# Outer term loop in split products, and separate issue of an expert's two weight transfers

## The chip, the cores and the metric

The kernel runs on one core of a Trainium2 chip. The metric is the device time of one execution in microseconds (us), the median of several executions. A core has five engines that run their own instruction streams in order and wait for each other by semaphores: TensorE (PE: matmuls, with PEld for its weight loads), VectorE (DVE), ScalarE (ACT), GpSimd (POOL) and SyncE (SP), which here issues nearly all DMA transfers.

## What is computed

Three layers follow one another: attention in which only scores close to the row's maximum count, a mixture of eight experts of which each token uses one, and a dense layer that all tokens pass.

```python
def _moe_ref(x, modality_id, w_gate, modality_bias, w1, w2):
    logits = x @ w_gate + modality_bias[modality_id]
    e_idx = np.argmax(logits, axis=1)
    ...
    for e in range(E):
        mask = e_idx == e
        h = np.maximum(x[mask] @ w1[e], 0.0)
        out[mask] = gate_w[mask, None] * (h @ w2[e])

def _moe2_ref(x, w_in, w_out):
    h = x @ w_in
    g = h * (1.0 / (1.0 + np.exp(-1.702 * h)))
    return g @ w_out
```

There are 2304 tokens of width 512. Each of the eight experts has w1 of 512 x 1024 and w2 of 1024 x 512; the dense layer has w_in of 512 x 2048 and w_out of 2048 x 512. All is fp32.

## The kernel before

**Split products.** Each fp32 operand of a product is split in two parts: a high part, rounded to the type that TensorE multiplies in one pass (float32r), and a low part, the rest. A product is then three terms: high weights with high data, high weights with low data, low weights with high data. ScalarE makes the high part (a copy that rounds), VectorE the low part (a subtraction that needs the high part).

**Expert blocks.** Tokens are sorted by expert into blocks of up to 512 rows, each of one expert. Five blocks stand in the program: four of 512 tokens and one of 264 (`SLOT_ROWS`, blocks 0 to 4 here; the code calls them slots). A block has eight steps, f = 0 to 7 (main loop, lines 1370 to 1416). Step f calls `ffn.step` (line 1025):

- `s1` (line 967), the first product: four pieces of 128 input channels (kd) times three terms, 12 matmuls of 128x128 weights with 512 columns of data (264 in the last block) into one accumulator, `tr`. Weights are ah (high) and al (low), data xh and xl.
- relu and its split, on ScalarE (hh) and VectorE (hl).
- `s2` or, in an expert block, `s2_cols` (line 1008), the second product, of the step two before (`LAG`): four groups of 128 output channels (d), each with an accumulator of its own, times three terms. Weights are bh and bl, data hh and hl.

The second product of a block's last step falls into step 1 of the next block. Behind it four evictions bring the accumulators to tiles y, and SyncE writes these to DRAM (lines 1273 and 1281).

**Weights.** They come in four pieces, g = 0 to 3, each for two steps. A piece has two transfers of 512 KB: ra (of w1, line 1227) and rb (of w2, line 1230), with two buffers each. `split(g, 0)` turns ra into ah and al (lines 1237 and 1238), `split(g, 1)` turns rb into bh and bl. At even f the loop splits the next piece's ra, `split(g + 1, 0)`, which step f + 2 uses; at odd f it splits rb of the current piece, which the second product uses in the next step. `load(g)` issues both transfers together, at odd f, two pieces ahead:

```python
            else:
                if f > 1 or not HO:
                    blk["split"](g, 1)
                if g + 2 < 4:
                    blk["load"](g + 2)
                elif nxt:
                    nxt["load"](g - 2)
```

At f = 1 `split(0, 1)` is called from inside the step (`mid`), between the first product and relu. A transfer into a buffer waits on SyncE until the split of the piece that held it is over; what stands behind it in SyncE's queue waits too.

**Other work in the same stretch.** `gather_slot` fetches the next block's rows (GpSimd), `scale` multiplies them by the gate's weight (ScalarE), `xprep` transposes and splits them, one of four pieces at a time, at the steps that `XP` gives; in blocks 0 and 1 the fourth piece comes at the very end of step 7. From block 1 on, `conv` prepares the dense layer's weights: a load of 512 KB into one of two buffers cv_raw (line 1138) in the steps that `CV` lists, ScalarE's and VectorE's bit operations one step later (from line 1144 on), and the split another step later.

**Dense layer.** Five blocks of tokens (four of 512 and one of 256) take 16 steps each, with `s1` as above on weights wi_h, wi_l and, in `s2`, h as weights and wo_h, wo_l as data (line 1000).

Of the kernel before, what the change touches and what calls it, by code (L numbers as in the profile page):

```python
# [33 lines left out]
CO = (0, 3)  # L34
CA = (0, 1, 2, 2, 2, 2, 2, 2, 2, 2, 2, 2, 2, 2, 2, 2)
CB = (0, 0, 0, 1, 0, 1, 0, 1, 0, 1, 0, 1, 0, 0, 0, 0)
HO = True
XP = ((0, 0, 0, 0, 1, 1, 1, 9), (0, 0, 0, 0, 1, 1, 1, 9), (0, 0, 0, 1, 1, 1, 9, 0))
SC = ((0, 0, 2, 2), (0, 0, 0, 4), (0, 0, 4, 0))
CV = ((), (3, 5, 7), (0, 1, 3, 4, 5, 7), (0, 1, 3, 4, 5, 7), ())  # L40
# [882 lines left out]
class Ffn:  # L923
# [43 lines left out]
    def s1(self, blk, f, mid):  # L967
        nc = self.nc
        T = blk["T"]
        wh, wl = blk["wa"](f)  # L970
        hps = self.ps_tr.tile([128, 512], F32, name="tr")
        i = 0
        for kd in range(4):
            for w, x in ((wh, "xh"), (wh, "xl"), (wl, "xh")):
                nc.tensor.matmul(hps[:, 0:T], w[:, kd, :], blk[x][:, kd, 0:T], start=(i == 0), stop=(i == 11))  # L975
                i += 1
        hh = self.hp.tile([128, 512], F32R, name="hh")
        hl = self.hp.tile([128, 512], F32R, name="hl")
        if mid:
            mid()  # L980
        self.pend.append((blk, f, hh, hl))
        return blk["act"](hps[:, 0:T], hh[:, 0:T], hl[:, 0:T])
# [25 lines left out]
    def s2_cols(self, blk, f, hh, hl):  # L1008

        nc = self.nc  # L1010
        T, last = blk["T"], blk["nf"] - 1
        if f == 0:
            sc = [self.ps_sc.tile([128, 2, 512], F32, name="sc") for _ in range(2)]
            blk["y"] = [sc[d // 2][:, d % 2, 0:T] for d in range(4)]
        wh, wl = blk["wb"](f)
        for d in range(4):
            ds = slice(d * 128, (d + 1) * 128)
            for i, (w, h) in enumerate(((wh, hh), (wl, hh), (wh, hl))):
                nc.tensor.matmul(  # L1019
                    blk["y"][d], w[:, ds], h[:, 0:T], start=(f == 0 and i == 0), stop=(f == last and i == 2))  # L1020
        if f == last:
            for d in range(4):
                blk["cols"](d, blk["y"][d])
# [16 lines left out]
def moe_kernel(ctx, tc, kq, v, tau, mid, w_gate, mod_bias, w1, w2, w_in, w_out, out):  # L1040
# [89 lines left out]
    ffn = Ffn(tc, ident, ps)  # L1130
# [81 lines left out]
    def slot(e_idx, g_rows, raw_tile, w_tile, put):  # L1212

        ev = nc.sync.value_load(e_idx, min_val=0, max_val=NE - 1)
        W = {}

        def scale(t, fast=False):

            g = g_rows[t]
            if fast:  # L1220
                nc.vector.tensor_scalar_mul(g[:, 0:DM], g[:, 0:DM], g[:, DM:DM + 1])
            else:
                nc.scalar.activation(g[:, 0:DM], g[:, 0:DM], ACTF.Copy, scale=g[:, DM:DM + 1])

        def load(g):
            ra = raw_tile("ra", "p (k f) -> p k f", dict(k=4))
            nc.sync.dma_start(
                ra, w1[bass.ds(ev, 1), :, g * 256:(g + 1) * 256].rearrange("a (kd p) f -> p (a kd) f", p=128))
            rb = raw_tile("rb", "p (g d) -> p g d", dict(g=2))
            nc.sync.dma_start(  # L1230
                rb, w2[bass.ds(ev, 1), g * 256:(g + 1) * 256, :].rearrange("a (g p) d -> p (a g) d", p=128))
            W[g] = [ra, rb]

        def split(g, i):
            raw = W[g][i]
            hi, lo = (w_tile("ab"[i] + x, ("p (k f) -> p k f", "p (g d) -> p g d")[i], (dict(k=4), dict(g=2))[i]) for x in "hl")
            nc.scalar.copy(hi, raw)  # L1237
            nc.vector.tensor_sub(lo, raw, hi.bitcast(F32))  # L1238
            W["ab"[i], g] = [hi, lo]

        def cols(d, yps):
            y, write = put(d, yps.shape[1])
            if d % 2:
                nc.vector.tensor_copy(y, yps)
            else:
                nc.scalar.copy(y, yps)
            if write:
                write(y)

        return dict(  # L1250
            nf=8, act=relu, cols=cols, scale=scale, load=load, split=split,
            wa=lambda f: [w[:, :, (f % 2) * 128:(f % 2) * 128 + 128] for w in W["a", f // 2]],
            wb=lambda f: [w[:, f % 2, :] for w in W["b", f // 2]],
        )
# [9 lines left out]
    blocks = {}  # L1264
# [91 lines left out]
        return blk, ffn.xsplit(blk, x_p, cols, w)  # L1356

    xq = make_slot(0)
    blocks[0]["load"](0)
    blocks[0]["load"](1)  # L1360
    att.tail(5)
    for t in range(SLOT_TILES[0]):
        blocks[0]["scale"](t, True)
    for i, f in enumerate(xq):
        f()
        att.tail(2)
        if i == 1:
            blocks[0]["split"](0, 0)
    conv, xq, gq = None, [], []
    for s in range(NS):  # L1370
        blk = blocks[s]
        for f in range(8):
            ffn.step(blk, f, (lambda: blk["split"](0, 1)) if f == 1 and HO else None, mid3=lambda: att.sides(6))
            f0 = F0[min(s, 2)]
            if s + 1 < NS and f in (f0, f0 + 1):
                if f == f0:
# [16 lines left out]
            if f % 2 == 0:  # L1393
                if g + 1 < 4:
                    blk["split"](g + 1, 0)
                elif nxt:
                    nxt["split"](0, 0)
            else:
                if f > 1 or not HO:
                    blk["split"](g, 1)  # L1400
                if g + 2 < 4:
                    blk["load"](g + 2)
                elif nxt:
                    nxt["load"](g - 2)
            if conv is None:
                if not att.tail(6):
                    open_resident()
# [33 lines left out]
    with tc.For_i(lo, hi, 1) as i:  # L1441
# [29 lines left out]
        for g in ffn.xprep(blk, x_p, g_rows):  # L1471
            g()
        for g in range(4):
            blk["load"](g)
            blk["split"](g, 0)
            blk["split"](g, 1)
            for f in (2 * g, 2 * g + 1):
# [70 lines left out]
```

## Time and profile before

| | us |
|---|---|
| median of three runs | 960.91 |
| lowest and highest | 960.05, 962.36 |
| the profiled execution | 962.34 |
| its span, first to last instruction | 960.6 |

The profile is of one execution. Attention fills it up to about 315 us, the expert blocks from 315 to 545, the dense layer from 545 to 950. In the timeline a matmul's length overlaps the next one's, so its pace is read from the starts. An idle time in brackets stands before the instruction named, with what ended it.

### The profile page before, as it was taken

What the parts mean: (1) busy time and instruction counts of PE and PEld (TensorE: products, weight loads), DVE (VectorE), ACT (ScalarE), POOL (GpSimd) and SP (SyncE); (2) the same over time, 40 slices, a digit from 0 to 9 for tenths busy, and PEclk for the clock granted to TensorE, in tenths of its full rate; (3) what the DMA queues carried; (4) which work ended last, traced back from release to release, by engine and by line L of the source; (5) the groups of instructions that cost most, each with busy time, mean ns of one, the idle gap of its engine ahead of it and who ended that gap; (6) DMA issues with size and microseconds to landing.
All of it is one profiled execution on the core that took longest, in us unless ns stands there. A gap on an engine that the chain in (4) does not pass through costs nothing.

```text
span 960.6 us, 13951 instructions
## 1 busy us (share of the span) xinstructions
PE 917.0 (95%) x5015; PEld 738.8 (77%) x5015; DVE 515.2 (54%) x1129; ACT 454.5 (47%) x820; POOL 224.8 (23%) x299
## 2 busy tenths in 40 slices
PE   8899999999988999899998999999999999999995
PEld 7777777777765778687877988888888888888894
DVE  6888888888896383578675578721211111111110
ACT  6777777777775442555444455422222222322221
POOL 4946475476413401010510000010001000100100
PEclk9999999999999999999999999999999999999998
DMA  7655855645405335455655244410001000100100
GB/s 222 153 141 154 227 160 128 180 121 139 112 2 160 103 101 179 151 201 195 202 186 198 76 162 135 132 44 1 23 22 45 6 12 6 44 1 1 44 1 25
DMA packets 64523, 100.71 MB, mean 105 GB/s; under 512 B 10597, under 2 KB 35971, under 8 KB 64451
## 3 DMA queue, kind: packets, MB, share of 16 engines
q1 hardware_dynamic: 61138, 89.84, 32.0%
q0 software_dynamic: 3312, 9.94, 3.2%
q8 instruction: 42, 0.69, 0.3%
q14 instruction: 31, 0.25, 0.1%
HBM read 63.97 MB, written 17.11 MB: 84 GB/s over the span
## 4 chain that ended last, share of the span: by engine, by line
PE 70%; DVE 10%; issue 8%; DMA 6%; ACT 3%; POOL 1%; SPq 1%; POOLq 0%; ACTq 0%; DVEq 0%
PE tr L975 24%; PE sc L1000 19%; PE sc L240 9%; PE sc L1019 6%; PE av L354 4%; PE tr L308 4%; DVE e L251 3%; DVE E L281 2%; DMA cv_raw<-in_moe_w_in_dram 2%; DMA ra<-in_moe_w_dram 2%; DMA xg<-x_dram,igaA 1%; PE tr L384 1%; DVE bl L1238 1%; PE av L350 1%; ACT e L257 1%
## 5 line engine op out<-in xcount | busy, mean ns | idle before, releaser
L1210 DVE TENSOR_TENSOR hl<-sg,hh 128x512 fp32r<-128x512 f32 (+1 forms) x80 | 51.1, 638 | 271.2 <-ACT hh L1208 271.2
L1207 ACT ACTIVATE sg<-tr 128x512 f32<-128x512 f32 (+1 forms) x80 | 44.3, 554 | 239.8 <-PE tr L975 236.7
L251 DVE TENSOR_SCALAR_CACHE_REDUCE e<-sc,taue 128x576 f32<-128x576 f32 x144 | 116.6, 813 | 30.3 <-PE sc L240 25.1
L257 ACT ACTIVATE e<-e,thr 128x576 f32<-128x576 f32 x144 | 111.3, 776 | 27.1 <-DVE e L251 26.5
L975 PE MATMUL tr<-xh,wi_l 128*128 128x512 f32 (+1 forms) x320 | 119.4, 373 | 0.0
L975 PE MATMUL tr<-xl,wi_h 128*128 128x512 f32 (+1 forms) x320 | 119.4, 373 | 0.0
L975 PE MATMUL tr<-xh,wi_h 128*128 128x512 f32 (+1 forms) x320 | 119.1, 372 | 0.0
L240 PE MATMUL sc<-kA,qT 128*128 128x288 f32 x320 | 102.2, 336 | 14.3 <-DVE E L281 11.1
L1000 PE MATMUL sc<-wo_h,hh 128*128 128x512 f32 x288 | 114.1, 396 | 0.0
L1000 PE MATMUL sc<-wo_h,hl 128*128 128x512 f32 x288 | 113.9, 396 | 0.0
L1000 PE MATMUL sc<-wo_l,hh 128*128 128x512 f32 x288 | 113.8, 395 | 0.0
L281 DVE SCALAR_TENSOR_TENSOR E<-sc,thr,e 128x576 f32<-128x576 f32 x128 | 103.7, 815 | 8.4 <-ACT e L257 4.1
L310 ACT COPY AT<-tr 128x512 f32<-128x512 f32 x128 | 73.9, 577 | 39.6 <-PE tr L308 39.5
L240 PE MATMUL sc<-kB,qT 128*128 128x288 f32 x320 | 89.3, 295 | 0.8 <-DVE kB L221 0.8
L240 PEld LDWEIGHTS sc<-kA,qT 128*128 128x128 f32 x320 | 60.2, 188 | 31.1 <-issue 19.4
L308 PE MATMUL tr<-ident,E 128*128 128x128 f32 x512 | 76.7, 272 | 0.0
L354 PE MATMUL av<-AT,V 128*64 128x288 f32 x512 | 76.7, 419 | 0.0
L975 PEld LDWEIGHTS tr<-xl,wi_h 128*128 128x128 f32 x320 | 60.1, 188 | 12.4
L975 PEld LDWEIGHTS tr<-xh,wi_h 128*128 128x128 f32 x320 | 60.1, 188 | 12.4
L975 PEld LDWEIGHTS tr<-xh,wi_l 128*128 128x128 f32 x320 | 60.3, 188 | 11.6
L975 PE MATMUL tr<-xh,ah 128*128 128x512 f32 (+1 forms) x160 | 61.8, 386 | 5.3 <-ACT ah L1237 4.6
L1000 PEld LDWEIGHTS sc<-wo_h,hl 128*128 128x128 f32 x288 | 54.2, 188 | 13.2
(219 smaller groups left out, 1701.4 us busy)
## 6 DMA issues: line engine op xcount, KB each, us to landing
ra<-in_moe_w_dram SPq DMA_DIRECT2D x20, 512.0 KB, 5.9
rb<-in_moe_w_dram SPq DMA_DIRECT2D x20, 512.0 KB, 4.4
F<-in_kq_dram SPq DMA_DIRECT2D x15, 640.0 KB, 5.0
cv_raw<-in_moe_w_in_dram SPq DMA_DIRECT2D x16, 512.0 KB, 5.1
cv_raw<-in_moe_w_out_dram SPq DMA_DIRECT2D x16, 512.0 KB, 4.0
V<-in_vp_dram SPq DMA_DIRECT2D x16, 320.0 KB, 4.5
kA<-kA SPq DMA_DIRECT2D x15, 320.0 KB, 3.3
kB<-kB SPq DMA_DIRECT2D x15, 320.0 KB, 3.4
```

What stands on the lines that cost most here:

```text
L240: nc.tensor.matmul(sc[:, hf, 0:288], l, d[kk][:, c0 + hf * 288:c0 + (hf + 1) * 288], start=(i == 0), stop=(i == len(ops) - 1),)
L251: nc.vector.tensor_scalar(e, d["sc", w][:, :, 0:288], self.taue[:, 0:1], 3.0e38, op0=ALU.add, op1=ALU.min, accum_out=thr)
L257: self.nc.scalar.activation(d["e", w], d["e", w], ACTF.Exp, bias=d["thr", w][:, 0:1], scale=-1.0)
L281: nc.vector.scalar_tensor_tensor(out=E.rearrange("p (a c) -> p a c", a=2), in0=d["sc", w][:, :, 0:288], scalar=d["thr", w][:, 0:1], in1=d[ ...
L308: nc.tensor.transpose(tp[:, kc * 128:(kc + 1) * 128], E[:, k0 + kc * 128:k0 + (kc + 1) * 128], self.ident)
L310: copies.append(lambda: nc.scalar.copy(AT[:, h, :, c * 128:(c + 1) * 128], tp.rearrange("p (k c) -> p k c", k=4)))
L354: nc.tensor.matmul(d["av"][h * 64:(h + 1) * 64, 0:288], d["V"][:, h, kc, :], d["AT"][:, h, kc, hf * 288:(hf + 1) * 288], start=False, stop ...
L975: nc.tensor.matmul(hps[:, 0:T], w[:, kd, :], blk[x][:, kd, 0:T], start=(i == 0), stop=(i == 11))
L1000: nc.tensor.matmul(y, h[:, cs], w, start=(f == 0 and i == 0), stop=(f == blk["nf"] - 1 and i == 2))
L1019: nc.tensor.matmul(blk["y"][d], w[:, ds], h[:, 0:T], start=(f == 0 and i == 0), stop=(f == last and i == 2))
L1207: nc.scalar.activation(sg, hps, ACTF.Gelu_apprx_sigmoid)
L1210: return [upper, lambda: nc.vector.tensor_sub(hl, sg, hh.bitcast(F32))]
```

## The change

Three edits:

1. `s1` and `s2_cols` loop over the three terms outside and over kd or d inside. The order of the terms in the second product is now bh with hh, bh with hl, bl with hh; the low part of the weights is last in both products. `s1` serves the dense layer too; `s2`, with which the dense layer makes its second product, is unchanged.
2. `load(g, i)` issues one of the two transfers. ra is loaded at even f, behind the split that reads the buffer's last content, three pieces ahead; rb at odd f, two pieces ahead as before. At f = 1 the load of rb is called right behind `split(0, 1)`, inside the step. ra of block 0's piece 2 is loaded ahead of the loop.
3. The constant `HO` goes, which was always true.

```diff
-        for kd in range(4):
-            for w, x in ((wh, "xh"), (wh, "xl"), (wl, "xh")):
+        for w, x in ((wh, "xh"), (wh, "xl"), (wl, "xh")):
+            for kd in range(4):
                 nc.tensor.matmul(hps[:, 0:T], w[:, kd, :], blk[x][:, kd, 0:T], start=(i == 0), stop=(i == 11))
                 i += 1
...
-        for d in range(4):
-            ds = slice(d * 128, (d + 1) * 128)
-            for i, (w, h) in enumerate(((wh, hh), (wl, hh), (wh, hl))):
+        for i, (w, h) in enumerate(((wh, hh), (wh, hl), (wl, hh))):
+            for d in range(4):
+                ds = slice(d * 128, (d + 1) * 128)
                 nc.tensor.matmul(
                     blk["y"][d], w[:, ds], h[:, 0:T], start=(f == 0 and i == 0), stop=(f == last and i == 2))
...
-        def load(g):
+        def load(g, i):
+            if i:
+                return load_b(g)
             ra = raw_tile("ra", "p (k f) -> p k f", dict(k=4))
             nc.sync.dma_start(
                 ra, w1[bass.ds(ev, 1), :, g * 256:(g + 1) * 256].rearrange("a (kd p) f -> p (a kd) f", p=128))
+            W[g] = [ra, None]
+
+        def load_b(g):
             rb = raw_tile("rb", "p (g d) -> p g d", dict(g=2))
             nc.sync.dma_start(
                 rb, w2[bass.ds(ev, 1), g * 256:(g + 1) * 256, :].rearrange("a (g p) d -> p (a g) d", p=128))
-            W[g] = [ra, rb]
+            W[g][1] = rb
...
     conv, xq, gq = None, [], []
+    blocks[0]["load"](2, 0)
     for s in range(NS):
         blk = blocks[s]
         for f in range(8):
-            ffn.step(blk, f, (lambda: blk["split"](0, 1)) if f == 1 and HO else None, mid3=lambda: att.sides(6))
+
+            def load_next(g, i):
+                b = blk if g < 4 else blocks.get(s + 1)
+                if b:
+                    b["load"](g % 4, i)
+
+            def second():
+                blk["split"](0, 1)
+                load_next(2, 1)
+
+            ffn.step(blk, f, second if f == 1 else None, mid3=lambda: att.sides(6))
...
                     blk["split"](g + 1, 0)
                 elif nxt:
                     nxt["split"](0, 0)
-            else:
-                if f > 1 or not HO:
-                    blk["split"](g, 1)
-                if g + 2 < 4:
-                    blk["load"](g + 2)
-                elif nxt:
-                    nxt["load"](g - 2)
+                load_next(g + 3, 0)
+            elif f > 1:
+                blk["split"](g, 1)
+                load_next(g + 2, 1)
```

The rows below are the instructions of the built programs in their order. Only TensorE's and SyncE's orders differ; those of ScalarE, VectorE and GpSimd are the same in both.

TensorE, the end of a first product (`tr`) and the start of the second product behind it (`sc`), in an expert block. Before, the last piece kd and the first group d:

```order
L975 MATMUL tr<-xh,ah 128x512
L975 MATMUL tr<-xl,ah 128x512
L975 MATMUL tr<-xh,al 128x512
L1019 MATMUL sc<-hh,bh 128x512
L1019 MATMUL sc<-hh,bl 128x512
L1019 MATMUL sc<-hl,bh 128x512
```

Now, the whole of both products:

```order
L974 MATMUL tr<-xh,ah 128x512 x4
L974 MATMUL tr<-xl,ah 128x512 x4
L974 MATMUL tr<-xh,al 128x512 x4
L1018 MATMUL sc<-hh,bh 128x512 x4
L1018 MATMUL sc<-hl,bh 128x512 x4
L1018 MATMUL sc<-hh,bl 128x512 x4
```

All twelve matmuls of each product are still there; al and bl are read by the last four of them, and the first four need all four pieces of xh.

SyncE at step 1 of block 2, from the last writes of block 1's output on (`y_first`). `eiB` is the read of the next block's expert number. Before, ra and rb of piece 2, a conversion load, then ra of piece 3:

```order
L1273 DMA y_first_77<-y_5248 128x512
L1273 DMA y_first_77<-y_5251 128x512
L1273 DMA y_first_77<-y_5254 128x512
L1214 TENSOR_LOAD eiB_4555
L1214 ISA x2
L1227 ISA
L1227 DMA ra_5276<-in_moe_w1_dram 128x4x256
L1230 ISA
L1230 DMA rb_5278<-in_moe_w2_dram 128x2x512
L1138 DMA cv_raw_5280<-in_moe2_w_in_dram 128x4x256
L1227 ISA
L1227 DMA ra_5372<-in_moe_w1_dram 128x4x256
```

Now rb of piece 2 is ahead of the four writes:

```order
L1234 DMA rb_5235<-in_moe_w2_dram 128x2x512
L1277 DMA y_first_77<-y_5251 128x512
L1277 DMA y_first_77<-y_5254 128x512
L1277 DMA y_first_77<-y_5257 128x512
L1277 DMA y_first_77<-y_5260 128x512
L1213 TENSOR_LOAD eiB_4557
L1213 ISA x2
L1137 DMA cv_raw_5282<-in_moe2_w_in_dram 128x4x256
L1228 ISA
L1228 DMA ra_5332<-in_moe_w1_dram 128x4x256
L1234 ISA
L1234 DMA rb_5376<-in_moe_w2_dram 128x2x512
```

Behind the writes there stand now the expert number and the conversion load; the ra behind them is block 3's first (at f = 2), and the rb is piece 3's (at f = 3).

SyncE at steps 3 to 5 of the same block. Before, rb of piece 3, then the conversion loads of f = 3 and f = 4, then block 3's first ra and rb at f = 5:

```order
L1230 ISA
L1230 DMA rb_5374<-in_moe_w2_dram 128x2x512
L1138 DMA cv_raw_5376<-in_moe2_w_in_dram 128x4x256
L1138 DMA cv_raw_5420<-in_moe2_w_in_dram 128x4x256
L1227 ISA
L1227 DMA ra_5469<-in_moe_w1_dram 128x4x256
L1230 ISA
L1230 DMA rb_5471<-in_moe_w2_dram 128x2x512
```

Now, beginning with the same rb:

```order
L1234 ISA
L1234 DMA rb_5376<-in_moe_w2_dram 128x2x512
L1137 DMA cv_raw_5378<-in_moe2_w_in_dram 128x4x256
L1228 ISA
L1228 DMA ra_5422<-in_moe_w1_dram 128x4x256
L1137 DMA cv_raw_5424<-in_moe2_w_in_dram 128x4x256
L1234 ISA
L1234 DMA rb_5473<-in_moe_w2_dram 128x2x512
L1137 DMA cv_raw_5475<-in_moe2_w_in_dram 128x4x256
```

An ra (of block 3's piece 1, at f = 4) has come between the two conversion loads.

## Rows read from the trace of the kernel before

**Rows 1.** the page, busy time of each engine, its share and its instructions

```profile
PE 917.0 (95%) x5015; PEld 738.8 (77%) x5015; DVE 515.2 (54%) x1129; ACT 454.5 (47%) x820; POOL 224.8 (23%) x299
```

**Rows 2.** busy time by stage: engines in turn, then TensorE clock, DMA share, GB/s

```profile
315.00:545.00 230.00, 218.97 (x1065) 179.75 (x1062) 144.05 (x243) 104.45 (x164) 39.40 (x53) 0.98 0.50 165
545.00:950.00 405.00, 403.87 (x1833) 329.64 (x1831) 112.89 (x192) 122.97 (x221) 16.55 (x17) 1.00 0.12 41
```

**Rows 3.** TensorE's waits, 315 to 545 us: total us, times, longest

```profile
PE tr L975 <- ACT ah L1237: 4.6, 2, 3.5
PE sc L1019 <- DVE bl L1238: 4.0, 4, 1.7
PE tr L975 <- DVE al L1238: 1.0, 2, 0.5
```

**Rows 4.** timeline of TensorE around five stalls: start us, us, line, operation

```profile
339.79 0.40 PE L1019 MATMUL sc<-hh,bh 128*128 128x512 f32 x1
...
341.51 0.40 PE L1019 MATMUL sc<-hh,bh 128*128 128x512 f32 x1
...
384.57 0.40 PE L1019 MATMUL sc<-hl,bh 128*128 128x512 f32 x1
...
391.77 0.39 PE L1019 MATMUL sc<-hh,bh 128*128 128x512 f32 x1
...
438.02 0.40 PE L1019 MATMUL sc<-hh,bh 128*128 128x512 f32 x1
...
439.80 0.39 PE L1019 MATMUL sc<-hh,bh 128*128 128x512 f32 x1
...
484.53 0.40 PE L975 MATMUL tr<-xh,al 128*128 128x512 f32 x1
...
491.08 0.75 PE L947 MATMUL av<-ident,xg 128*128 128x128 f32 x3
...
523.02 0.28 PE L1019 MATMUL sc<-hl,bh 128*128 128x264 f32 x1
...
532.61 0.28 PE L1019 MATMUL sc<-hh,bl 128*128 128x264 f32 x1
```

**Rows 5.** busy time by stretch, blocks 3 and 4; columns as in rows 2

```profile
488.50:491.00 2.50, 2.50 (x7) 1.87 (x6) 1.23 (x2) 0.00 (x0) 0.00 (x0) 0.50 0.95 362
528.40:532.40 4.00, 4.00 (x19) 4.00 (x19) 2.49 (x4) 1.83 (x4) 0.00 (x0) 0.50 0.39 113
532.60:541.00 8.40, 8.40 (x72) 8.40 (x71) 4.91 (x8) 3.43 (x7) 0.00 (x0) 1.00 0.30 122
```

**Rows 6.** timeline of SyncE's queue, 300 to 550 us: start us, us, issue

```profile
375.87 0.39 SPq L1227 DMA_DIRECT2D ra<-in_moe_w_dram  x1
...
475.07 0.46 SPq L1138 DMA_DIRECT2D cv_raw<-in_moe_w_in_dram  x1
...
520.36 0.41 SPq L1227 DMA_DIRECT2D ra<-in_moe_w_dram  x1
```

**Rows 7.** timeline of ScalarE, blocks 1, 3, 4; in brackets idle time before

```profile
384.96 1.04 ACT L1237 CAST ah<-ra 128x1024 fp32r<-128x1024 f32 x1 [7.61 <-DMA ra<-in_moe_w_dram]
...
482.73 0.67 ACT L1144 ACTIVATE cv_a<-cv_raw 128x512 f32<-128x512 f32 x1 [2.09 <-DMA cv_raw<-in_moe_w_in_dram]
...
525.72 1.04 ACT L1237 CAST ah<-ra 128x1024 fp32r<-128x1024 f32 x1 [6.37 <-DMA ra<-in_moe_w_dram]
```

**Rows 8.** timeline at the start of block 2, VectorE and TensorE

```profile
414.27 0.68 DVE L949 SCALAR_TENSOR_TENSOR xl<-av,xh 128x512 fp32r<-128x512 f32 x1
...
415.58 0.40 PE L1019 MATMUL sc<-hh,bh 128*128 128x512 f32 x1
```

**Rows 9.** timeline of TensorE in the dense layer, one first product

```profile
712.67 0.40 PE L975 MATMUL tr<-xh,wi_h 128*128 128x512 f32 x1
712.91 0.39 PE L975 MATMUL tr<-xl,wi_h 128*128 128x512 f32 x1
713.14 0.40 PE L975 MATMUL tr<-xh,wi_l 128*128 128x512 f32 x1
```

More of the change, by code (lines that the diff above doesn't have):

```diff
@@ L36 @@
 CB = (0, 0, 0, 1, 0, 1, 0, 1, 0, 1, 0, 1, 0, 0, 0, 0)
-HO = True
 XP = ((0, 0, 0, 0, 1, 1, 1, 9), (0, 0, 0, 0, 1, 1, 1, 9), (0, 0, 0, 1, 1, 1, 9, 0))
@@ L1358, in moe_kernel @@
     xq = make_slot(0)
-    blocks[0]["load"](0)
-    blocks[0]["load"](1)
+    for g in range(2):
+        for i in range(2):
+            blocks[0]["load"](g, i)
     att.tail(5)
@@ L1473, in moe_kernel @@
         for g in range(4):
-            blk["load"](g)
+            for i in range(2):
+                blk["load"](g, i)
             blk["split"](g, 0)
```

## The prediction

> **What bounds the kernel now.** I read the page first: TensorE is busy 95% of the span [rows 1], so only time in which it stands still, or runs at half clock, can be won. The table by stage comes next [rows 2]. From 545 to 950 us (the dense layer) it is busy 403.87 of 405 us at full clock; the list of waits has no matmul that waits there. From 315 to 545 us (five expert blocks) it is busy 218.97 of 230 us at a clock of 0.98: 11 us of idle time, and some half clock. What the matmuls of that stretch wait for is nearly all one thing, expert weights [rows 3]: 4.6 us for ah (ScalarE's high copy of a w1 piece), 4.0 us for bl (VectorE's low part of a w2 piece), 1.0 us for al.
>
> A stall costs more than its idle time, so I take it from the starts of matmuls [rows 4]. Regular starts are 0.23 us apart with 512 columns [rows 9], and 0.12 us with the last block's 264 (72 matmuls in 8.40 us [rows 5]). Each pair of rows 4 is the last regular matmul before a stall and the first regular one after it:
> - A, block 0: three steps in 1.72 us; 1.72 - 0.69 = 1.03 us.
> - B, block 1: 16 steps (twelve of the first product, four of the second) in 7.20 us; 7.20 - 3.68 = 3.52 us.
> - C, block 2: three steps in 1.78 us; 1.09 us.
> - D, block 3: 13 steps (twelve of the second product and the transposes behind it) in 6.55 us; 3.56 us.
> - E, block 4: 23 steps (twelve and eleven) of 0.12 in 9.59 us; 6.83 us.
>
> Together 16.03 us. D and E hold the half clock too: in 488.5 to 491 and 528.4 to 532.4 us the granted clock is 0.50, the lower level of 1.2 GHz, each after the longest idle times of the list, 1.7 and 3.5 us [rows 3, 5].
>
> **Where the stalls come from.** At f = 1 SyncE's queue holds the four y writes of the block before, which wait for that block's last product and its evictions, and behind them ra and rb of piece 2. In block 1 ra goes out at 375.87, in block 4 at 520.36 [rows 6]. ScalarE needs it one step later, stands 7.61 and 6.37 us before it and starts the copies at 384.96 and 525.72 [rows 7]: landings of 9.1 and 5.4 us. ScalarE works in order, so the relu and the bh copy behind it are late as well: B and E. In block 3 it is the conversion's cv_raw, issued at 475.07 behind the writes, ra and rb, used at 482.73 after a wait of 2.09 us [rows 6, 7]; behind it come relu, bh, bl, and D. C has the same order of instructions; A has SyncE held by writes of x rows ahead of ra.
>
> **The change, part by part.**
> *The earlier ra.* No transfer is added: 20 ra and 20 rb as before, on the same queue, and ScalarE, VectorE and GpSimd keep their order. Each ra now follows the split that frees its buffer, at even f, four steps ahead of its use instead of one. Four steps are 4 x 24 x 0.23 = 22 us (about 11.5 in block 4), against the worst landing of 9.1 us. So ah and al, and what queues behind ah on ScalarE, go: B and E, 10.35 us. The half clock after E goes with its idle time.
> *rb and cv_raw at f = 1.* rb of piece 2 is now ahead of the y writes; it waits for VectorE's split (0,1), and the writes, whose data are needed in the dense layer only, may go out a microsecond later at no cost. The cv_raw load stands directly behind the writes, without two 512 KB transfers ahead and one behind it. It needs to land 2 us sooner for D's wait to be gone, and those transfers took that or more of its 7.7 us. So C and D lose their cause.
> *Term order.* In the second product bl is first read by the ninth matmul instead of the second, 7 x 0.23 = 1.6 us later. That alone covers A, C and the bl part of B (overdue by about 1.0 us each), and all but 0.4 us of D (overdue by 2.0 us). hl, wanted at the fifth matmul, is two steps old. bh is still wanted at once.
> Saved: 16.03 us; each stall has at least one cover.
>
> *What term order costs.* In the first product the fourth piece of x is wanted earlier: high part at the fourth matmul instead of the tenth, low part at the eighth instead of the eleventh. At the start of block 2 its low part is made at 414.27 to 414.95 us, and the product gives way to the second one at 415.58 [rows 8]. Now five matmuls would follow it, 414.95 + 5 x 0.23 = 416.10: 0.5 us lost. Block 1 has the same schedule with an emptier VectorE: between 0 and 0.5, I take 0.1, since that copy is done about when it is wanted. Blocks 3 and 4 prepare the piece a step earlier, the dense layer many steps: 0. At the start of block 4 all four accumulators are touched within four matmuls, where the second pair used to come six matmuls, 0.7 us, after the first and so had that much longer to be evicted: 0 to 0.7, I take 0.3. Together 0.9 us. Alternating accumulators costs nothing: today's second product changes its accumulator after every third matmul with the same 0.23.
> *Net:* 16.0 - 0.9 = 15.1 us. The profiled execution took 962.34 us (span 960.6): 947.2. It stands 1.4 above the median of the runs, 960.91, so in their terms **945.8 us**. The dense layer runs back to back and passes the gain on.
>
> **Rivals.**
> *The stall moves to the conversion loads.* At f = 0 and f = 4 of blocks 2 and 3 a cv_raw load now stands behind an ra that waits for the split of the same step; before, it went out with the load ahead. ScalarE reads it a step, 5.5 us, later; landings were 5.4 to 9.1 us, so it could wait up to 3.6 us. Up to 1.8 us of that would reach the matmuls after the cover of the term order: four places, 7.2 us, 953.0; with a spell of half clock at each as in D (half of 2.5 us and a restart, some 1.4 us) 12.8 us, 958.6. For it: D came about in this way. Against: each transfer now stands nearly alone in its step. Chance 0.10.
> *No gain.* The time returns elsewhere, the dense layer's first steps waiting for conversions that no longer get 15 us of expert work as cover: up to all of 15.1 us, 960.9. Against: no matmul waits there now, and the conversions are paced by steps, not by time. Chance 0.04.
> *Slower: changed weights show their load.* In the first product two neighbouring matmuls shared their weights (wh with xh, then with xl); now none do. There are 480 such pairs (160 in the experts, 320 in the dense layer). If a change of weights cost more than 15.1 / 480 = 0.03 us, the kernel would be slower; with a load wholly exposed, 738.8 / 5015 = 0.15 us in the mean [rows 1], it would be 480 x 0.15 = 72 us, 1018 us. The rows speak against it: weights are loaded for every matmul already (5015 loads, 5015 matmuls [rows 1]), and a pair with equal weights takes 0.24 us from 712.67 to 712.91, the change behind it 0.23 us [rows 9]; at the rounding of 0.01 us per pair the sum moves by under 5 us. Chance 0.03. The Trainium skill, page TensorE: Matmul & The Clock Gate, section Packing small matmuls — row/col tiling, says that a weight load overlaps matmuls in flight only where it addresses another group of rows; by that, every full-height load would be exposed, and this would be the outcome. The starts 0.23 us apart with a load for each do not bear that out here.
>
> **How the numbers follow.** The forecast has 0.83 and by itself runs from 943.5 (all 16, none of the 0.9, and the scatter of a run) to 950 (4 us of A to D stay: a gather or a conversion is late instead). The range of 943.5 to 953 takes in the milder form of the first rival. A measurement can tell 0.2%, 1.9 us. Faster by more than that: the forecast, and the first rival in either form, 0.93. The same: 0.04. Slower: 0.03.
>
> **What would show it.** Right: the stretch from the first expert product to the dense layer is some 15 us shorter, the dense layer's 405 us is the same; in the list of matmul waits ah and bl are gone or below 1 us; no spell of half clock between 315 and 545 us; ScalarE no longer stands before ra; a wait for xl of half a microsecond at the start of block 2. Wrong: matmuls there waiting for bh behind cv_raw, first products whose matmuls start more than 0.24 us apart, or new idle time in the dense layer.

## The result and the profile after

The changed kernel takes 947.81 us (median of four executions, 946.41 to 948.91), the kernel before 961.63 in the four executions beside it (960.05 to 963.29). The ratio is 0.9855, 95% interval 0.9833 to 0.9878: 13.8 us faster. Forecast were 945.8, within 943.5 to 953. The profiled execution is the fastest of the four, 946.41 us (span 944.6), 15.9 us below the profiled one of before. The kernel before has that one trace, of 962.34 us, while its executions beside the experiments have medians of 959.24, 959.56 and 960.66 us (15, 15 and 17 of them), so that differences against its trace may be too large by some 2 us in all (an estimate from these four times).

Three views answer to rows 1 to 3. The page, busy time of each engine:

```profile
PE 910.1 (96%) x5015; PEld 734.9 (78%) x5015; DVE 516.2 (55%) x1129; ACT 455.0 (48%) x820; POOL 224.8 (24%) x299
```

The table by stage, cut where the changed kernel's first dense matmul starts (columns as in rows 2):

```profile
315.00:525.50 210.50, 208.94 (x1041) 173.65 (x1040) 143.30 (x242) 102.36 (x161) 38.45 (x52) 1.00 0.55 180
525.50:935.00 409.50, 407.40 (x1851) 332.63 (x1849) 114.17 (x193) 125.15 (x223) 17.23 (x18) 1.00 0.12 41
```

And all of TensorE's waits from 312 to 530 us (total us, times, longest):

```profile
PE tr L974 <- ACT xr L388: 0.7, 1, 0.7
PE tr L383 <- DVE hl L1198: 0.4, 1, 0.4
PE tr L722 <- POOL pre L688: 0.2, 1, 0.2
```

The number of instructions is the same on each engine. The expert stretch has 1.6 us of idle time instead of 11 [rows 2], at full clock throughout. Of the 9.6 us for ah, bl and al [rows 3] nothing is left; the three waits belong to attention and routing work that still runs in block 0.

The timeline of TensorE, its stretch boundaries (a row with xN stands for N matmuls):

```profile
314.99 0.97 PE L974 MATMUL tr<-xh,ah 128*128 128x512 f32 x3
...
525.60 0.86 PE L974 MATMUL tr<-xh,wi_h 128*128 128x512 f32 x3
```

From the first expert matmul to the first dense one it is 210.61 us (525.60 - 314.99); before, 225.86 (315.71 to 541.57, read in the same way). From there to the start of the last matmul it is 406.91 us, before 406.90. So of the 15.9 us between the two traces 15.25 lie in the expert blocks.

SyncE and ScalarE in block 1, the place of stall B:

```profile
366.54 0.37 SPq L1228 DMA_DIRECT2D ra<-in_moe_w_dram  x1
367.67 0.37 SPq L1234 DMA_DIRECT2D rb<-in_moe_w_dram  x1
373.06 2.14 SPq L1277 DMA_DIRECT2D y_first<-y  x4
378.48 0.40 SPq L1228 DMA_DIRECT2D ra<-in_moe_w_dram  x1
```

```profile
376.14 1.04 ACT L1241 CAST ah<-ra 128x1024 fp32r<-128x1024 f32 x1
```

No ra stands directly behind the writes any more; the one at 378.48 belongs to step 2. The copy to ah has no wait in brackets, where rows 7 had 7.61 us. But three parts of the change act together here, and this profile can't say which of them did it.

### The profile page after: what moved, and what is told of

Read it like the earlier page. It is cut to its first block, busy times and chain, and to the rows that moved or that the text cites. A ratio compares the mean times of both kernels' runs of the same rounds, so it can differ in the third digit from the quotient of the medians.

```text
span 944.6 us, 13971 instructions
## 1 busy us (share of the span) xinstructions
PE 910.1 (96%) x5015; PEld 734.9 (78%) x5015; DVE 516.2 (55%) x1129; ACT 455.0 (48%) x820; POOL 224.8 (24%) x299
## 4 chain that ended last, share of the span: by engine, by line
PE 77%; DVE 9%; issue 6%; ACT 3%; DMA 2%; POOL 1%; SPq 1%; POOLq 0%; ACTq 0%; DVEq 0%
PE tr L974 27%; PE sc L999 19%; PE sc L239 9%; PE sc L1018 8%; PE av L353 5%; PE tr L307 5%; DVE e L250 3%; DVE E L280 2%; PE tr L383 1%; PE av L349 1%; ACT e L256 1%; PE tr L328 1%; DVE bl L1242 1%; DMA cv_raw<-in_moe_w_in_dram 1%; PE av L946 1%
## 5 line engine op out<-in xcount | busy, mean ns | idle before, releaser
L974 PE MATMUL tr<-xh,wi_h 128*128 128x512 f32 (+1 forms) x320 | 80.8, 375 | 0.0
L974 PE MATMUL tr<-xl,wi_h 128*128 128x512 f32 (+1 forms) x320 | 80.3, 372 | 0.0
L974 PE MATMUL tr<-xh,wi_l 128*128 128x512 f32 (+1 forms) x320 | 80.1, 372 | 0.0
L974 PEld LDWEIGHTS tr<-xh,wi_h 128*128 128x128 f32 x320 | 57.8, 188 | 13.0
L974 PEld LDWEIGHTS tr<-xl,wi_h 128*128 128x128 f32 x320 | 56.9, 188 | 11.9
L974 PEld LDWEIGHTS tr<-xh,wi_l 128*128 128x128 f32 x320 | 56.8, 188 | 11.6
L999 PEld LDWEIGHTS sc<-wo_l,hh 128*128 128x128 f32 x288 | 54.3, 188 | 12.3
```

What stands on the lines that cost most here:

```text
L999: nc.tensor.matmul(y, h[:, cs], w, start=(f == 0 and i == 0), stop=(f == blk["nf"] - 1 and i == 2))
```

## The experiments

The measure that tells most is the length of the blocks, from the first matmul of one to the first of the next (block 4: to the first dense matmul), from the timeline of TensorE of each profiled execution. All in us; the dense part is 406.90 to 406.92 in every kernel.

| kernel | 0 | 1 | 2 | 3 | 4 | stretch |
|---|---|---|---|---|---|---|
| before | 46.07 | 50.73 | 47.19 | 49.13 | 32.75 | 225.86 |
| changed | 45.42 | 46.99 | 46.50 | 45.32 | 26.38 | 210.61 |
| e1 changed, again | 45.45 | 46.99 | 46.54 | 45.33 | 26.35 | 210.66 |
| e2 loads only | 45.55 | 46.83 | 45.88 | 45.31 | 25.99 | 209.56 |
| e3 order only | 45.72 | 50.95 | 47.43 | 47.28 | 30.49 | 221.87 |
| e4 loads, second product | 45.29 | 47.08 | 45.87 | 45.31 | 26.36 | 209.91 |
| e5 ra late | 49.46 | 49.82 | 49.20 | 46.91 | 35.63 | 231.01 |
| e6 rb late: early ra alone | 45.79 | 46.71 | 45.89 | 45.33 | 26.01 | 209.73 |
| e7 one step in new order | 45.54 | 46.87 | 45.86 | 45.32 | 26.33 | 209.92 |
| e8 two x pieces in a step | 50.16 | 53.19 | 45.79 | 45.32 | 26.52 | 220.97 |
| e9 y on GpSimd's queue | 45.39 | 46.74 | 50.48 | 52.07 | 26.21 | 220.89 |
| e10 ra at step 0 | 44.98 | 46.73 | 45.92 | 45.32 | 28.08 | 211.03 |
| e11 x a step earlier | 45.39 | 46.98 | 47.16 | 45.29 | 26.41 | 211.24 |

The same kernel twice (changed, e1) differs by 0.05 us here, while the times of its executions differ by up to 2.5. "A step takes" below means the time from the first matmul of a step's first product to that of the next step's.

My theory from the trace after: the early transfers do nearly everything. Its rival: the term order does it.

**e1, the changed kernel again.** No edit.

> The changed kernel itself, once more beside the others: the yardstick. 946 to 949 us, ratio to the kernel before 0.985, first expert product to first dense product 210.6 us (225.9 before).

948.64 us, ratio 0.9881 (0.9853 to 0.9909), which is 11.4 us below the kernel before; the stretch is the same. e2 to e4 ran beside it on the same chip.

**e2, the new transfers with the old order of terms.**

```diff
-        for w, x in ((wh, "xh"), (wh, "xl"), (wl, "xh")):
-            for kd in range(4):
+        for kd in range(4):
+            for w, x in ((wh, "xh"), (wh, "xl"), (wl, "xh")):
...
-        for i, (w, h) in enumerate(((wh, hh), (wh, hl), (wl, hh))):
-            for d in range(4):
-                ds = slice(d * 128, (d + 1) * 128)
+        for d in range(4):
+            ds = slice(d * 128, (d + 1) * 128)
+            for i, (w, h) in enumerate(((wh, hh), (wl, hh), (wh, hl))):
```

> The new transfers with the old order of terms in both products. My theory: the transfers alone win nearly everything. Expert stretch 210.6 us within 0.7: the small new losses at the starts of blocks 1, 2 and 4 (0.9 us) go, and one wait for bl of about 0.6 us comes in step 0 of block 0, the only place where bl of the changed kernel is made later than the old order wants it. No waits for ah. Rival, that the term order does the work and the transfers little: waits for bl of 0.5 to 2 us return in blocks 0 to 3, and the stretch is 215 us or longer.

947.47 us, ratio 0.9867 (0.9839 to 0.9895); stretch 209.56, even 1.1 below the changed kernel. The one wait for weights in TensorE's list is the one that was expected:

```profile
PE sc L1018 <- DVE bl L1242: 0.4, 1, 0.4
```

The transfers alone win all of it, and the kernel with the term order is 1.1 us longer. Its four executions (946.94 to 948.00) lie below the four of e1 (948.16 to 949.45); a ratio to the kernel before can't tell 0.1%, the traces can.

**e3, the old transfers with the new order of terms.** The kernel before with the first part of the change and nothing else:

```diff
-        for kd in range(4):
-            for w, x in ((wh, "xh"), (wh, "xl"), (wl, "xh")):
+        for w, x in ((wh, "xh"), (wh, "xl"), (wl, "xh")):
+            for kd in range(4):
...
-            for i, (w, h) in enumerate(((wh, hh), (wl, hh), (wh, hl))):
+        for i, (w, h) in enumerate(((wh, hh), (wh, hl), (wl, hh))):
+            for d in range(4):
```

> The old transfers with the new order of terms in both products. My theory: stalls A, C and most of D go (bl, al), B and E stay in their main part, which is ah: waits for ah of 3.5 to 4.6 us, none for bl over 0.5, half clock in block 4 as before. Stretch 218 to 220 us, time 953 to 956 us. Rival, that the term order does the work: stretch 211 to 213 us, like the changed kernel.

957.78 us, ratio 0.9984 (0.9969 to 1.0000): hardly a gain. The stretch is 221.87, 4.0 below the one trace of before instead of 6 to 8 (the medians differ by 1.5), so the expectation of 218 to 220 missed, on the far side from the rival; the waits for ah are below the 3.5 to 4.6 us expected. TensorE's waits, 305 to 535 us:

```profile
PE tr L975 <- ACT ah L1237: 2.9, 2, 1.6
PE av L947 <- DVE xl L949: 2.7, 3, 1.2
PE sc L1019 <- ACT bh L1237: 1.2, 2, 0.9
```

The waits for bl are gone, as was meant. A wait for xl, three times, stands in their place. Block 1 shows how it comes: ScalarE, VectorE, then TensorE.

```profile
385.19 1.04 ACT L1237 CAST ah<-ra 128x1024 fp32r<-128x1024 f32 x1 [7.77 <-DMA ra<-in_moe_w_dram]
```

```profile
396.93 0.43 DVE L1145 TENSOR_SCALAR cv_e<-cv_raw 128x512 uint32<-128x512 uint32 x1 [3.82 <-DMA cv_raw<-in_moe_w_in_dram]
...
399.48 0.68 DVE L949 SCALAR_TENSOR_TENSOR xl<-av,xh 128x512 fp32r<-128x512 f32 x1
```

```profile
400.22 0.65 PE L947 MATMUL av<-ident,xg 128*128 128x128 f32 x4 [1.10 <-DVE xl L949]
```

ra lands late, so ah, bh and bl are late; the next rb waits for their buffer, and the conversion load behind it goes out at 391.82 us in SyncE's queue. VectorE reads that load at 396.93, and then makes xl; the next transposition needs the accumulator av that xl reads. In the kernel before VectorE makes the same xl at 399.44, 0.04 earlier. This chain of transfers runs beside the matmuls, and the time that the term order saves at bl is paid at xl: block 1 is no shorter (50.95 against 50.73). Blocks 2 and 3 show both halves. Step 4, where bl was late, falls from 7.04 to 5.94 us in block 2 and from 9.66 to 6.41 in block 3; step 5, where xl is now waited for, grows from 5.96 to 6.59 and from 5.84 to 7.23.

**e4, the new transfers, the new order in the second product alone.** The changed kernel with the old loop in `s1`:

```diff
-        for w, x in ((wh, "xh"), (wh, "xl"), (wl, "xh")):
-            for kd in range(4):
+        for kd in range(4):
+            for w, x in ((wh, "xh"), (wh, "xl"), (wl, "xh")):
```

> The new transfers, the new order in the second product alone, the old order in the first. My theory: the losses at the starts of blocks 1 and 2 (0.26 and about 0.5 us) go, the one at block 4 (0.3) stays, nothing else changes: stretch 209.9 us, 0.7 below the changed kernel, dense layer 406.9 us as it is. Rival, that the order of the first product itself has a price or a gain, by changed weights at 480 pairs: dense layer other than 406.9 by more than 1 us.

947.37 us, ratio 0.9868 (0.9840 to 0.9896); stretch 209.91 and dense part 406.92, both as expected. So the order of the first product costs the 0.7 us, nearly all of it in block 2 (45.87 against 46.54). TensorE at the start of block 2, in the changed kernel:

```profile
407.40 1.42 PE L974 MATMUL tr<-xh,ah 128*128 128x512 f32 x4
408.66 1.46 PE L974 MATMUL tr<-xl,ah 128*128 128x512 f32 x4
409.96 0.63 PE L974 MATMUL tr<-xh,al 128*128 128x512 f32 x2
```

Its twelve starts take 3.26 us there and 2.88 in block 1; with the old order (e2, e4) 2.6 in both. Block 1 of e4 is no shorter for it: its step 5 takes 6.29 us, in e1 5.96, and why was not followed. Changed weights at each matmul cost nothing: the dense part, with 320 of the 480 pairs, didn't move.

Which of the transfers is it, then, and why was it late? Three kernels ask that.

**e5, ra late.** e2 with the ra of piece 2 at the end of step 1 (two lines that only keep the tiles are left out):

```diff
-    blocks[0]["load"](2, 0)
...
-                load_next(g + 3, 0)
+                if f == 2:
+                    load_next(3, 0)
+                if f in (2, 4):
+                    load_next(g + 3, 0)
             elif f > 1:
                 blk["split"](g, 1)
                 load_next(g + 2, 1)
+            else:
+                load_next(2, 0)
```

> The kernel of e2 (new transfers, old order of terms) with the ra of piece 2 issued at the end of step 1 again, behind the four y writes, and the ra of piece 3 at step 2; rb stays ahead of the writes. My theory: it is the early ra that wins. The ScalarE waits for ra return, with them stalls A, B, C and E (1.0, 3.5, 1.1, 6.8 us) and the half clock in block 4; D returns in part, since one transfer instead of two stands ahead of its conversion load. Stretch 219 to 224 us against 209.6. Rival, that the place of rb and of the conversion load wins: stretch below 213.

965.61 us, ratio 1.0059 (1.0041 to 1.0077): slower than before. The stretch of 231.01 is above my range. The waits are those of rows 3, and larger:

```profile
PE tr L974 <- ACT ah L1241: 8.1, 3, 5.8
PE sc L1018 <- DVE bl L1242: 3.7, 3, 1.7
PE tr L974 <- DVE al L1242: 2.0, 4, 0.5
```

The place of ra, with rb where e5 has it, is worth 21.5 us (231.01 - 209.56), more than the whole gain. What I had missed: the rb of piece 2 is now ahead of ra, and in three blocks ra is in use later after its issue. In block 2, for one, rb goes out at 426.40 and ra at 430.71, and ScalarE starts ah at 436.77, 6.1 us later; before, ra went out at 427.66 with rb, a conversion load and another ra within 1.7 us behind it, and ah started at 431.12, 3.5 us later. The same in blocks 0 (5.6 against 3.5) and 4 (6.7 against 5.4), not in blocks 1 (8.6 against 9.1) and 3 (5.6 against 5.4). That the rb is the reason is not shown: e3, with the transfers in the order of before, has 3.8 us in block 4 where before has 5.4, so that the time varies without it. Half clock comes with the two longest waits, of 1.8 us in block 0 and 5.8 in block 4; the second line begins inside the wait, which ends at 531.48 (columns as in rows 2):

```profile
340.20:343.40 3.20, 3.20 (x8) 2.52 (x9) 3.03 (x12) 1.54 (x2) 0.00 (x0) 0.50 0.50 164
528.00:538.00 10.00, 6.07 (x26) 5.76 (x27) 5.03 (x7) 4.63 (x7) 0.00 (x0) 0.50 0.40 139
```

In block 3 ScalarE waits for ra alone and not for the conversion load behind it, and the block is 1.6 us longer than in e2:

```profile
484.05 1.05 ACT L1241 CAST ah<-ra 128x1024 fp32r<-128x1024 f32 x1 [3.55 <-DMA ra<-in_moe_w_dram]
...
485.57 0.69 ACT L1143 ACTIVATE cv_a<-cv_raw 128x512 f32<-128x512 f32 x1
```

**e6, rb late.** e2 with the rb of piece 2 where it was before, so that of the whole change only the early ra is left:

```diff
             def second():
                 blk["split"](0, 1)
-                load_next(2, 1)
...
-            elif f > 1:
-                blk["split"](g, 1)
+            else:
+                if f > 1:
+                    blk["split"](g, 1)
                 load_next(g + 2, 1)
```

> The kernel of e2 with the rb of piece 2 issued at the end of step 1, behind the y writes and ahead of the conversion load; ra stays early. My theory: rb is used four steps later and hides; the conversion load gets one transfer ahead of it and lands later by 1 to 2 us, which costs up to 1 us in block 3 and nothing elsewhere. Stretch 209.6 to 210.6. The prediction's step, that rb's place removes C and D, would want 1.1 + 3.6 us back: 214.

947.12 us, ratio 0.9874 (0.9851 to 0.9897); stretch 209.73. The early ra alone is the gain. Against before, the blocks are shorter by 0.28, 4.02, 1.30, 3.80 and 6.74 us, and C and D are gone with it, though rb stands ahead of D's conversion load as it did before. Block 3, SyncE and ScalarE:

```profile
467.96 0.41 SPq L1234 DMA_DIRECT2D rb<-in_moe_w_dram  x1
468.41 0.47 SPq L1137 DMA_DIRECT2D cv_raw<-in_moe_w_in_dram  x1
```

```profile
473.81 0.67 ACT L1143 ACTIVATE cv_a<-cv_raw 128x512 f32<-128x512 f32 x1 [1.78 <-DMA cv_raw<-in_moe_w_in_dram]
```

The conversion load still keeps ScalarE waiting, 1.78 us against 2.09 [rows 7], but sooner in the block. With one transfer ahead of it instead of two, it goes out 14.3 us after the block's start instead of 15.4 (468.41 - 454.15, 475.07 - 459.69), and ScalarE reads it at 19.7 instead of 23.0. ScalarE comes to it sooner too: before, it had waited 2.96 us for ra just ahead (at 479.07). In the kernel before the load was the later of the two, and D came from it, by way of VectorE's queue, to TensorE:

```profile
482.67 0.43 DVE L1145 TENSOR_SCALAR cv_e<-cv_raw 128x512 uint32<-128x512 uint32 x1 [0.69 <-DMA cv_raw<-in_moe_w_in_dram]
...
485.84 1.21 DVE L1238 TENSOR_TENSOR bl<-rb,bh 128x1024 fp32r<-128x1024 f32 x1
```

```profile
487.11 0.50 PE L1019 MATMUL sc<-hh,bl 128*128 128x512 f32 x1 [1.73 <-DVE bl L1238]
```

**e9, y on GpSimd's queue.** The kernel before, loads and terms untouched, with the writes of y (and the read of their place, two lines in `rest`) on `nc.gpsimd`:

```diff
-                nc.sync.dma_start(y_first[d * 128:(d + 1) * 128, j * PG:j * PG + w], y)
+                nc.gpsimd.dma_start(y_first[d * 128:(d + 1) * 128, j * PG:j * PG + w], y)
```

> The kernel before, with one edit: the four writes of a block's output y are issued by GpSimd instead of SyncE. Loads, their order and the order of terms stay as before. My theory, that the ra of piece 2 is late only because it stands in SyncE's queue behind writes that wait for a product: in blocks 1 to 4 ra goes out up to 12 us sooner, right behind the rb ahead of it, and B, C, D and E go (15 us of the 16), A stays (there x rows are written, not y). Stretch 210 to 213 us. Rival, that the transfers are late because ra and rb are issued as a pair and share the DMA engines: stretch stays above 220.

961.70 us, ratio 1.0019 (1.0006 to 1.0032); stretch 220.89, outside my 210 to 213 and where the rival wanted it. (The profiled execution, 959.71 us, is the fastest of twelve, and from its last matmul's start to the end of the span it takes 14.6 us instead of 12.1.) As a whole neither is right: the stretch hides two opposite things. Where the theory spoke of ra it held: in block 1 ra goes out at 361.17, 0.5 us after the block's start, where before it was 14.1 (375.87 - 361.78), and blocks 1 and 4 are as short as in e6 (46.74 and 26.21). That is 10.5 us, without a load moved: B and E come from SyncE's queue standing behind writes that wait for a product. (A stays, but with 0.4 us instead of 1.0, though block 0 has no write of y: step 4 takes 6.22 us, before 6.90, in e2 and e6 5.85. A stall's size is not the same in every execution.) Blocks 2 and 3 became 3.3 and 2.9 us longer, because GpSimd's queue now stands behind the same writes. GpSimd in block 1:

```profile
372.43 1.90 POOL L1273 DMA_DIRECT2D y_first<-y  x3 [15.07 <-ACT y L1246]
...
375.44 1.08 POOL L1062 DMA_INDIRECT xg<-x_dram,igaB  x1 [0.38 <-issue]
```

The gathers of the next block's rows come behind it. In block 2 ScalarE waits for such rows (`scale`), and ah, behind it on ScalarE, is late once more; block 3 is like it:

```profile
429.37 1.36 ACT L1223 ACTIVATE xg<-xg 128x512 f32<-128x512 f32 x2 [5.80 <-DMA xg<-x_dram,igaB]
430.64 1.03 ACT L1237 CAST ah<-ra 128x1024 fp32r<-128x1024 f32 x1
```

TensorE's waits of e9, 305 to 560 us:

```profile
PE av L947 <- ACT xg L1223: 2.3, 2, 2.0
PE sc L1019 <- DVE bl L1238: 1.6, 1, 1.6
PE tr L975 <- ACT ah L1237: 1.2, 2, 0.6
```

**e10, ra at step 0.** e6 with a short lead, but ahead of the writes:

```diff
-                load_next(g + 3, 0)
+                if f == 0:
+                    load_next(2, 0)
+                if f in (2, 4):
+                    load_next(g + 3, 0)
+                if f == 2:
+                    load_next(3, 0)
```

(The ra of block 0's piece 2 ahead of the loop goes too.)

> The kernel of e6 (early ra, rb and order of terms as before) with the ra of piece 2 issued at step 0 instead of step 6 of the block before, which is ahead of the y writes, but 9 us instead of 20 us ahead of its use; the ra of piece 3 at step 2. My theory, that the place ahead of the writes decides: landings of 4 to 6 us fit into it, stretch 209.7 to 211 us. Rival, that the long lead decides (landings reach 9.1 us): waits for ah in blocks 1 and 4 of 1 to 3 us each, stretch 213 us or more.

948.40 us, ratio 0.9873 (0.9856 to 0.9891); stretch 211.03. Blocks 1 to 3 are the same as with the long lead: the place ahead of the writes decides. Block 4, whose steps are half as long, loses 2.1 us against e6, at the ra of piece 3, which now stands behind its y writes:

```profile
508.92 3.78 SPq L1285 DMA_DIRECT2D y_rest<-y  x4
512.91 0.41 SPq L1234 DMA_DIRECT2D rb<-in_moe_w_dram  x1
513.52 0.41 SPq L1228 DMA_DIRECT2D ra<-in_moe_w_dram  x1
```

```profile
520.27 1.05 ACT L1241 CAST ah<-ra 128x1024 fp32r<-128x1024 f32 x1 [2.53 <-DMA ra<-in_moe_w_dram]
```

Block 0 wins 0.8 us against e6, which shows a price of the early ra. In e6 the ra of piece 3 goes out half a microsecond ahead of the writes of x rows, and GpSimd waits longer for such a write. Behind it come ScalarE's bh, VectorE's bl and TensorE (step 2 takes 6.44 us, in e10 5.49). GpSimd and TensorE in e6, then GpSimd in e10, where this ra comes later:

```profile
325.96 0.61 POOL L391 TENSOR_TENSOR xrow<-xr,r 128x256 f32<-128x256 f32 x1 [2.90 <-DMA x_dram<-xrow]
```

```profile
329.46 0.50 PE L1018 MATMUL sc<-hh,bl 128*128 128x512 f32 x1 [0.67 <-DVE bl L1242]
```

```profile
327.04 0.61 POOL L391 TENSOR_TENSOR xrow<-xr,r 128x256 f32<-128x256 f32 x1 [1.73 <-DMA x_dram<-xrow]
```

In all eight kernels with an ra there this GpSimd instruction starts 9.9 to 10.2 us after the block's first matmul, in the other five 9.0 to 9.1.

**Attempts at a faster kernel: e7, e8, e11.** e7 is e2 with a branch in `s2_cols`, of which these are the lines that change the order:

```diff
+        if f == 0 and blk.get("first"):
+            order = [(d, i) for i in (0, 2, 1) for d in range(4)]
```

> The kernel of e2 with the new order of terms in the second product of block 0's step 0 alone, where e2 waits for bl: 0.7 us (two starts of 0.82 and 0.33 us for 0.23) go, nothing else changes. Stretch 208.9 us, time 0.7 below e2. Rival, that the wait comes back at the next reader of VectorE's work: stretch 209.6 as e2.

947.67 us, ratio 0.9869 (0.9846 to 0.9893); no gain. Block 0 is as long as in e2 (45.54 against 45.55): TensorE no longer waits for bl there, but 0.3 us for routing results from GpSimd (pre), for which e2 doesn't wait (step 3 takes 6.46 us, in e2 5.76). The rival held in its number; the wait that came is one for GpSimd, not for VectorE as I wrote.

e8 and e11 change the table of x pieces in the changed kernel. e8:

```diff
-XP = ((0, 0, 0, 0, 1, 1, 1, 9), (0, 0, 0, 0, 1, 1, 1, 9), (0, 0, 0, 1, 1, 1, 9, 0))
+XP = ((0, 0, 0, 0, 1, 1, 9, 0), (0, 0, 0, 0, 1, 1, 9, 0), (0, 0, 0, 1, 1, 1, 9, 0))
```

> The changed kernel with the fourth piece of x prepared one step earlier in blocks 0 and 1 (as it is in blocks 2 and 3). My theory: the waits for xl at the starts of blocks 1 and 2 go, 0.8 us: stretch 209.8 us. Rival, that these starts wait for something else: stretch 210.6.

957.12 us, ratio 0.9977 (0.9962 to 0.9991); stretch 220.97, 10.3 longer than e1. No first product waits for xl in the list any more, but my edit did more than I wrote: it puts two pieces into step 6, and there is one accumulator av. The second transposition waits until VectorE, behind al and other work, has read the first:

```profile
359.22 1.12 PE L946 MATMUL av<-ident,xg 128*128 128x128 f32 x4 [2.93 <-DVE xl L948]
```

After each of the two waits there is a spell at half clock. The table by stretch, behind the first and the second:

```profile
359.00:362.30 3.30, 3.08 (x10) 2.60 (x11) 0.86 (x2) 0.59 (x1) 0.00 (x0) 0.50 0.35 66
412.00:416.90 4.90, 4.90 (x14) 3.84 (x13) 0.69 (x1) 0.59 (x1) 3.57 (x4) 0.50 0.43 112
```

e11 has one piece in each of steps 3 to 6:

```diff
+XP = ((0, 0, 0, 1, 1, 1, 9, 0), (0, 0, 0, 1, 1, 1, 9, 0), (0, 0, 0, 1, 1, 1, 9, 0))
```

> The changed kernel with the four pieces of x at steps 3, 4, 5 and 6 in blocks 0 and 1, one in each, as blocks 2 and 3 have them (e8 put two into step 6, where the second waited for the one accumulator). My theory: the waits for xl at the starts of blocks 1 and 2 (0.8 us) go: stretch 209.8. Rival: block 1 begins to gather a step later than block 2 does, so its first piece waits for the gathered rows: stretch 211 or more.

948.49 us, ratio 0.9875 (0.9857 to 0.9893); stretch 211.24, no gain, and for neither reason. The first products at the starts of blocks 1 and 2 take 2.52 us each instead of 2.88 and 3.26, and nothing waits for gathered rows. But in block 2 a conversion load is late, VectorE with it, and the transposition behind it, which takes 1.4 us more:

```profile
440.05 0.43 DVE L1144 TENSOR_SCALAR cv_e<-cv_raw 128x512 uint32<-128x512 uint32 x1 [3.51 <-DMA cv_raw<-in_moe_w_in_dram]
...
442.62 0.68 DVE L948 SCALAR_TENSOR_TENSOR xl<-av,xh 128x512 fp32r<-128x512 f32 x1
```

In the changed kernel VectorE reads the same load after a wait of 0.90 us, at 437.25. Block 2's own table is the same in both; why the load is late there wasn't followed.

The best kernels are e2, e4 and e6 (947.1 to 947.5 us, stretch 209.6 to 209.9). They beat both given ones in the traces, the changed one by about 1 us in 948. No run joins block 0 of e10 with the rest of e6; by the table that would be 0.8 us less again (an estimate).

## Why the prediction was right, and where not

**The size.** Forecast were 16.03 us saved and 0.9 lost, net 15.1; from one trace to the other the stretch got 15.25 shorter. In the medians of four and four it is 13.8 (11.7 to 16.1 by the interval), and 11.4 by the ratio of e1 beside fifteen executions of the kernel before. So 15 us is the gain over the one execution from which the stalls were read; by the medians it is some 11 to 14. The prediction took that execution's stalls for the median's, and so its saving is some 1 to 4 us too large as one for the median.

**The stalls.** That a stall costs its late starts rather than its idle time held: e6 takes out 16.13 us, where the list of waits had 9.6 [rows 3]. By block it is 0.28, 4.02, 1.30, 3.80 and 6.74, forecast 1.03, 3.52, 1.09, 3.56 and 6.83 [rows 4]. A itself was sized right: its step falls from 6.90 us to 5.85, and e10 wins 1.09 in block 0. What the prediction put at nothing is the price of the early ra there, a later GpSimd and behind it a wait for bl (0.95 us in e6, e10 shows how it comes) or, in the changed kernel, one for GpSimd's results (0.4: step 3 takes 6.35 us, before 5.95).

**The cause of B and E.** "The four y writes ... and behind them ra": e9 shows it by moving the writes alone, e10 by the place alone, e5 by putting ra back. The early ra was given 10.35 us; blocks 1 and 4 of e6 won 10.76.

**First failed step: "rb and cv_raw at f = 1 ... So C and D lose their cause".** The load was rightly named, the credit to rb was not. e6 leaves rb in its old place, ahead of the conversion load, and C and D are gone all the same. Taking the ra from ahead of the load was enough: in block 3 ScalarE reads it 3.4 us sooner after the block's start (19.7 against 23.0; in block 2 19.9 against 22.3), where the prediction asked for 2; with rb away too, in the changed kernel, it is 19.3. The late ra also held ScalarE itself, 2.96 us, which the prediction did not look at. Alone, with no wait at the load behind it, such a hold costs 1.6 us in block 3 (e5). How D's 3.8 us divide between these two ways of the same ra no run shows.

**Second failed step: "That alone covers A, C and the bl part of B, and all but 0.4 us of D".** Alone, the term order wins 0.35 in block 0, loses 0.2 in each of blocks 1 and 2, and wins 1.85 in block 3 and 2.26 in block 4 (e3); in block 4 ra was also in use 1.5 us sooner after its issue than before (3.8 against 5.4), so that gain may not be the order's. At its own step the cover worked in blocks 2 and 3 about as forecast, for A only in part (6.90 to 6.53 us); one step later a part came back. I had taken a matmul's lateness for a quantity that a cover consumes. It belonged to VectorE's queue, and the next reader of that queue paid it. Beside the early ra the order has next to nothing left to cover, and in the first product it costs 0.7 us (e4 against e1). The prediction came out right because both failed steps were second covers for stalls that the early ra removed anyway. For A, C and D, 5.7 us of the 16.03, that is luck.

**The costs.** The start of block 2 was put at 0.5, block 1 at 0.1; the first products there are 0.64 and 0.27 us longer than in e2. The 0.3 at block 4's start can't be laid to the order: it comes with the new order (e1, e4) but also with the old (e7, a start of 0.50 us at 511.39), and is absent with the old one in e2 and e6.

**The rivals.** Changed weights: 406.91 against 406.90 us in the dense part; out. No gain: out. The stall at the conversion loads did not come in the changed kernel; ScalarE waits for them, 1.42 us in block 3 for one, and no matmul waits behind it. e11, one step of x away, has it, 1.4 us in one place, so its chance of 0.10 was not for nothing.

## What to carry to other kernels

Look first for what stands ahead of a late transfer in its issuing queue. Here writes that waited for a result held every load behind them, and moving the writes to another queue moved the hold to what stood there. Before a trace's stalls are added up into a forecast, ask how far that execution lies from the median. Hiding a late operand from one reader gains little if the engine that makes it stays late: find that engine's next product and who waits for it. When several parts of a change cover the same loss, try each alone; here one of three was the gain, one was idle and one had a price.

## What was not expected of the hardware

- The same transfer takes very different times. From issue to use by a ScalarE that waits for it, the 512 KB ra of piece 2 took 3.5, 9.1, 3.5, 5.4 and 5.4 us in blocks 0 to 4 of the kernel before, and 3.7, 8.7, 3.5, 3.9 and 3.8 in e3, which issues the same transfers in the same order. What decides is not shown.
- Half clock after waits in the experts, in the rows: 2.93 and 3.51 us idle in e8, then 0.50, where matmuls start 0.43 us apart; the same after the wait of 2.0 us for xg in e9 (483.8 to 490.6 us). With it e8 lost 4.7 us in block 0 and 6.2 in block 1, at that one idle time in each.
- Undisturbed first products with 512 columns take 2.52 us from the first start to the twelfth in the experts, 0.229 us a matmul, and starts in the dense layer are 0.233 us apart (699.73 to 701.83 us, nine steps), at the same clock of 1.00 and in both orders of terms. Why the dense layer is 2% slower per matmul stays open. Over its 406.9 us it would be some 7 us (an estimate).
